# Hash projection on eighths of the matmul array, weight rounding one unit ahead, and a third buffer for loaded q and k

## The chip, the cores and the metric

The kernel runs on one core of a Trainium2 chip. The metric is the device time of one execution in microseconds. Before the change the median of three runs is 935.21 us (933.5 to 935.66).

## The reference

The program is an attention block with a hash mask, followed by an MLP. In NumPy, cut to what matters:

```python
# q, k, v: (4, 8, 768, 64) float32; proj: (64, 6)
q_bits = einsum(q, proj) > 0;  k_bits = einsum(k, proj) > 0     # 6 bits per row
mask   = bucket(q_bits)[:, :, :, None] == bucket(k_bits)[:, :, None, :]
attn   = softmax(where(mask, q @ k.T / 8, -1e9));  y = attn @ v
x = y.transpose(0, 2, 1, 3).reshape(3072, 512)
h = x @ w_in                                   # w_in (512, 2048)
out = (max(h, 0) + alpha * min(h, 0)) @ w_out  # w_out (2048, 512)
```

A query row attends to the key rows whose six hash bits all agree with its own. The MLP weights arrive as 64-bit floats and are rounded to float32 in the kernel.

## The kernel before, in words

**Two stages.** The attention stage takes the first 370 us or so; the MLP stage takes the rest. In the attention stage the 32 heads of the batch are taken as 16 pairs (`pi`), and each pair as two units (`u = 2 * pi + g`, with `g` 0 or 1 for the half of the 384 query columns). The loop at L1002 runs over the 32 units. Every engine's order is the order of the program (`do` at L439 keeps it), so an instruction that has to wait holds up everything behind it on its engine. Which DMA is issued when on a queue is left to the scheduler.

**One unit on TensorE.** `scores` (L687) runs six key chunks: three for the second half of unit `u`, and then three for the first half of unit `u + 1`. Each chunk is a bf16 product of hash bits and a float32 product of q and k, added in PSUM (L696), for the two heads `s` of the pair; each head occupies 64 rows of the array. After them comes either `hash_bits(pi + 1)` (L1016, in units with `g == 0`) or the transposes of q and k for pair `pi + 2` (`turn`, L1018 and L1019, in units with `g == 1`). Then comes the first half of `attend` (L729), `totals` (L741), and the second half of `attend`.

**Where the PSUM results go.** ScalarE takes the exponential of every score chunk (L701), copies the transposes (L648), writes the hash bits as signs (L676), takes the absolute value of a weight piece for rounding (`weight_abs`, L558) and sums squares of q and k (`magnitude`, L657). VectorE sums probabilities over key chunks (L710, L715, L716, L719; one of the six chunks is added by a DMA, L711), does the rounding of one weight piece per unit (`weight_parts`, L564 to L569, `weight_sum`, L589 and L594), the sums of weight blocks that the MLP's Strassen products need (`weight_sums`, L614), and the division (`divide`, L751 to L757). `totals` on TensorE needs L719 of its unit. `divide` needs `totals` and both halves of `attend`.

**The hash.** `hash_bits` (L659) multiplies the 6-column projection with the transposed q and k of both heads. The weight of head `s` (`wh[s]`, L457) has 128 rows, of which the 64 rows of the other head are zero. A product therefore uses all 128 rows and 32 columns of the array. For each half of the 768 columns there are four products: k and q of head 0, k and q of head 1. They land in the four 32-partition groups of one PSUM bank.

```python
r = D * s + 32 * n
do(PE.matmul(ps[r : r + 32, half, :CW], wh[s],
             tr[name, pi][:, half * CW : (half + 1) * CW], start=True, stop=True))
```

**Weights.** There are 32 pieces (`NW`), one rounded per unit. In unit `u` the kernel rounds piece `u`: `weight_abs(u)` stood at the end of the unit before, `weight_parts(u)` stands ahead of the first half of `attend`, and `weight_sum(u)` after `totals`. Pieces form groups; when a group is complete (`weight_group`) four sums and a store to DRAM are queued, and `weight_sums` takes one or two of them per unit. In the last unit `weight_sums(4)` (L1028) takes what is left. The first MLP activations are written by L849 into a pool that takes the place of the attention stage's pool in SBUF, so this write has to wait for the last readers of what lay there.

**Loads.** `load` (L479) fetches q, k and v of a pair. The tiles for q and k rotate over two buffers; the load for pair `pi + 2` overwrites what `magnitude(pi)` has just read. L1044 to L1050 place the magnitudes and the loads that follow them. All of these loads, the weight pieces and most stores are issued on the SyncE queue.

Of the kernel before, what the change touches and what calls it, by code (L numbers as in the profile page):

```python
# [404 lines left out]
def fast_path(  # L405
# [48 lines left out]

    ident = const.tile([P, P], F32, name="ident")
    ones = const.tile([P, D], F32, name="ones")
    wh = [const.tile([P, 32], F32, name=f"wh{s}") for s in range(2)]  # L457
    hb = const.tile([P, 1], F32, name="hb")
    alpha16 = const.tile([NF, P], F32, name="alpha16")
    alpha = const.tile([P, NF], F32, name="alpha")  # L460
# [18 lines left out]
    def load(pi, name):  # L479
        b, hp = pairs[pi]  # L480
        src = {"q": q, "k": k, "v": v}[name]
        if name == "v":
            t = pool.tile([P, 2, NC * D], F32, name=f"vn{pi}", tag="vn")
            nc.sync.dma_start(t, src[b, 2 * hp : 2 * hp + 2].rearrange("h (p c) d -> p h (c d)", c=NC))
            nat[name, pi] = t
        else:
            load_part(pi, name, slice(0, NC), nc.sync)

    def load_part(pi, name, cs, queue):
        b, hp = pairs[pi]  # L490
        src = {"q": q, "k": k}[name]
        if cs.start == 0:
            nat[name, pi] = pool.tile([P, NC, 2, D], F32, name=f"{name}n{pi}", tag=f"{name}n")
        for s in range(2):
            queue.dma_start(nat[name, pi][:, cs, s], src[b, 2 * hp + s].rearrange("(p c) d -> p c d", c=NC)[:, cs])

    def setup():

        zero = const.tile([P, 512], BF16, name="zero")
        do(DVE.memset(zero, 0.0))  # L500
        for s in range(2):
            do(DVE.memset(wh[s], 0.0))
            nc.sync.dma_start(wh[s][D * s : D * s + D, :NB], proj)
        nc.sync.dma_start(alpha16, moe_alpha.rearrange("(t p) -> t p", p=P))
        make_identity(nc, ident)
        do(DVE.memset(ones, 1.0))

        ps = psum.tile([P, 512], F32, name="nil", tag="av")
        for i in range(12):
            do(PE.matmul(ps, zero[:, :P], zero, start=True, stop=True))  # L510

        do(DVE.memset(hb, 0.0))
        for r in range(0, P, 32):
            do(DVE.memset(hb[r : r + 2 * NB], 1.0 if r % D else -1.0))
            do(DVE.memset(hb[r : r + NB], -1e-37))
# [39 lines left out]
    def weight_abs(i):  # L555
        lo, hi = halves(i)
        wx[i] = pool.tile([P, 512], F32, name=f"wx{i}", tag="wx")
        do(ACT.activation(wx[i], hi.bitcast(F32), AF.Abs))  # L558

    def weight_parts(i):  # L560
        lo, hi = halves(i)
        x = wx[i]
        wr[i] = r = pool.tile([P, 512], F32, name=f"wr{i}", tag="wr", bufs=1)
        do(DVE.tensor_scalar(x, x, HI_MIN, None, op0=ALU.max, op1=ALU.max, accum_out=wmax[:, i : i + 1]))  # L564
        do(DVE.tensor_scalar(
            x.bitcast(U32), x.bitcast(U32), 3, 0xC0000000, op0=ALU.logical_shift_left, op1=ALU.bitwise_xor,
        ))
        do(DVE.tensor_scalar(r.bitcast(U32), x.bitcast(U32), 0x7F800000, None, op0=ALU.bitwise_and))
        do(DVE.scalar_tensor_tensor(r, lo, 2.0 ** -52, r, op0=ALU.mult, op1=ALU.mult))  # L569

    def weight_sum(i):


        lo, hi = halves(i)
        x, r = wx[i], wr[i]
        if i < HW:
            n, m = divmod(i, 4)
            if m == 0:
                wst[n] = pool.tile([P, NM, 4, P], F32, name=f"wsi{n}", tag="wsi")
# [79 lines left out]
    def hash_bits(pi, halves=BOTH):  # L659


        if halves.start == 0:
            bits["q", pi] = qbs[pi % 2]
            bits["k", pi] = pool.tile([P, S], BF16, name=f"kb{pi}", tag="kb")
        ps = two_banks(f"hs{pi}")
        for half in range(halves.start, halves.stop):
            for s in range(2):
                for n, name in enumerate("kq"):
                    r = D * s + 32 * n
                    do(PE.matmul(  # L670
                        ps[r : r + 32, half, :CW], wh[s], tr[name, pi][:, half * CW : (half + 1) * CW],
                        start=True, stop=True,
                    ))

        def sign(t, rows, ps_rows):
            do(ACT.activation(  # L676
                t[rows].rearrange("p (h w) -> p h w", h=2)[:, halves], ps[ps_rows, halves, :CW], AF.Sign,
                bias=hb[ps_rows],
            ))

        for s in range(2):
            sign(bits["q", pi], slice(D * s, D * s + 32), slice(D * s + 32, D * s + D))

        sign(bits["k", pi], slice(0, P), slice(0, P))


    def scores(u, half):  # L687
        pi, g = divmod(u, NCH)
        qs = slice(g * CW, (g + 1) * CW)
        for kc in range(half * NC // 2, (half + 1) * NC // 2):  # L690
            sc = two_banks(f"sc{u}_{kc}")
# [9 lines left out]
            do(ACT.activation(pt[:, :, :CW], sc[:, :, :CW], AF.Exp, scale=SCALE / DOWN))  # L701
            prob[u, kc] = pt
# [290 lines left out]
    for i in range(1, 3):  # L993
        load_weight(i)
    load(1, "v")
    scores(0, 0)
    add_first(0)
    hash_bits(0, second)
    for name in "qk":
        turn(1, name)  # L1000
    weight_abs(0)
    for u in range(UNITS):  # L1002
        pi, g = divmod(u, NCH)
        scores(u, 1)
# [12 lines left out]
        if g == 1 and pi + 2 < NPAIR:  # L1017
            turn(pi + 2, "q")  # L1018
            turn(pi + 2, "k")  # L1019
        weight_parts(u)  # L1020
        attend(u, 0)
        totals(u)
        weight_sum(u)
        weight_sums(1 if u < HW else 2)
        weight_group(u)
        attend(u, 1)
        if u == last:
            weight_sums(4)  # L1028
        divide(u)
        if g == 1 and pi + 2 < NPAIR:  # L1030
            load(pi + 2, "v")
        load_weight(u + 3)
        if u == HW + 2:
            load_w(0)
            load_w(1)
            load_x(0)
        if HW + 4 <= u < HW + 8:
            sum_x(0, u - HW - 4, DVE)
        if u + 1 < NW:
            weight_abs(u + 1)  # L1040
        if u == 1:
            setup_alpha()

        done = [(u, "q"), (u, "k")] if u < 2 else []  # L1044
        if 2 <= pi + 1 + g < NPAIR:
            done.append((pi + 1 + g, "kq"[g]))
        for p2, name in done:
            magnitude(p2, name)
            if p2 + 2 < NPAIR:
                load(p2 + 2, name)  # L1050


    late = []
# [83 lines left out]
```

## Time and profile before

The page of the profile shows these engines over the span of 932.4 us:

| engine | busy us | share |
|---|---|---|
| TensorE, matmul | 916.9 | 98% |
| VectorE | 756.1 | 81% |
| ScalarE | 399.6 | 43% |
| GpSimd | 40.9 | 4% |

The busy share is an average over stages. In the 40 slices of the span VectorE shows 9 tenths or more from slice 3 to slice 15, which is the attention stage, and ScalarE shows 6 to 8 tenths up to slice 14. In the MLP stage ScalarE falls to 1 to 3 tenths. The chain of work that ended last is 92% TensorE, 3% VectorE, 2% ScalarE and 1% DMA. A busy TensorE record is modelled and overlaps its neighbour: a float32 product of 384 columns is shown as 0.49 us, but such records follow each other every 0.325 us. The distance between starts is therefore the figure to use.

A pair of regular units takes 22.13 us in the chain. The unit from 306.09 to 317.15 us holds the scores (4.95 us), the hash (1.43 us), half of `attend` (2.09 us), the totals (0.65 us) and the other half (1.94 us).

### The profile page before, as it was taken

To read this page: it belongs to the slowest core of one execution; us is meant where nothing else is said; L and a number is where in the kernel's file an instruction comes from. 1 tells how busy PE (TensorE), PEld (TensorE's weight loads), DVE (VectorE), ACT (ScalarE), POOL (GpSimd) and SP (SyncE) were. 2 spreads that over 40 slices of the span, in tenths; PEclk is the share of its full clock that TensorE was granted. 3 is DMA by queue.
4 is the path that set the end of the run, shared out by engine and by line. 5 is a ranking of instruction groups with operands and counts; after the bars stand their busy time and mean duration, and the time that the engine had idled before them with its cause. 6 is when DMAs were issued, how large, how long until landed. Compare 5 with 4: busy or idle time off the path is not lost.

```text
span 932.4 us, 13579 instructions
## 1 busy us (share of the span) xinstructions
PE 916.9 (98%) x5073; PEld 610.5 (65%) x5073; DVE 756.1 (81%) x1317; ACT 399.6 (43%) x690; POOL 40.9 (4%) x50
## 2 busy tenths in 40 slices
PE   8999999999999999899999999999999999999996
PEld 4444444444454444556999556998556998556996
DVE  2889999999999999677978667988667988677985
ACT  6877777777777763222122222122222112322212
POOL 1111111111111110000000000000000000000000
PEclk9999999999999999999999999999999999999999
DMA  7876888989877563634424334334234334231231
GB/s 187 191 177 159 218 204 208 268 211 234 220 187 187 153 165 99 236 102 147 146 109 153 112 119 142 135 108 169 96 118 152 126 115 162 98 116 40 94 133 71
DMA packets 114062, 141.50 MB, mean 152 GB/s; under 512 B 54067, under 2 KB 102211, under 8 KB 110403
## 3 DMA queue, kind: packets, MB, share of 16 engines
q1 hardware_dynamic: 103680, 127.56, 43.2%
q0 software_dynamic: 8704, 12.58, 8.3%
q8 instruction: 42, 0.69, 0.3%
q10 hardware_dynamic: 1600, 0.39, 0.2%
q14 instruction: 36, 0.27, 0.1%
HBM read 100.67 MB, written 27.26 MB: 137 GB/s over the span
## 4 chain that ended last, share of the span: by engine, by line
PE 92%; DVE 3%; ACT 2%; DMA 1%; issue 1%; SPq 0%; DVEq 0%; ACTq 0%
PE sc L696 15%; PE av L729 12%; PE hs L670 2%; PE z_4a L803 2%; PE z_5a L803 2%; PE z_7a L803 2%; PE z_3a L803 2%; PE z_1a L803 2%; PE z_6a L803 2%; PE z_2a L803 2%; PE f_5a L803 2%; PE f_7a L803 2%; PE f_3a L803 2%; PE f_4a L803 2%; PE f_2a L803 2%; PE f_6a L803 2%
## 5 line engine op out<-in xcount | busy, mean ns | idle before, releaser
L701 ACT ACTIVATE pt<-sc 128x768 f32<-128x768 f32 x192 | 152.9, 814 | 78.5 <-PE sc L696 76.6
L696 PE MATMUL sc<-qT,kT 64*128 64x384 f32 x768 | 155.1, 483 | 0.0
L729 PE MATMUL av<-pt,vn 128*64 128x385 f32 (+1 forms) x768 | 136.5, 491 | 0.0
L729 PEld LDWEIGHTS av<-pt,vn 128*64 128x64 f32 x768 | 52.3, 136 | 70.7 <-issue 61.2
L696 PEld LDWEIGHTS sc<-qT,kT 64*128 64x128 f32 x768 | 68.2, 188 | 34.8 <-issue 34.4
L853 DVE TENSOR_TENSOR g<-g,g 128x384 f32<-128x384 f32 x128 | 68.4, 555 | 2.2
L696 PE MATMUL sc<-qb,kb 64*128 64x384 bf16 x384 | 63.0, 325 | 1.6 <-ACT kb L676 1.5
L893 DVE TENSOR_TENSOR ws<-wl 128x512 f32<-128x512 f32 x56 | 38.5, 688 | 23.4 <-DMA wl<-w_out_s 23.4
L901 DVE TENSOR_TENSOR gs<-g,gs 128x768 f32<-128x768 f32 x56 | 53.5, 955 | 1.0
L901 DVE TENSOR_TENSOR gs<-g 128x768 f32<-128x768 f32 x56 | 53.4, 953 | 0.0
L711 POOL DMA_DIRECT2D accp<-pt x32 | 38.5, 1204 | 317.0 <-DVE accp L710 189.4
L849 DVE SCALAR_TENSOR_TENSOR g<-h,alpha 128x384 f32<-128x384 f32 x32 | 19.8, 618 | 35.3 <-ACT h L842 35.3
L696 PEld LDWEIGHTS <-kb 64*128 64x128 bf16 x384 | 19.2, 94 | 41.7 <-issue 18.4
L715 DVE TENSOR_TENSOR accd<-pt,pt 128x768 f32<-128x768 f32 x32 | 30.6, 956 | 14.1 <-ACT pt L701 14.0
L710 DVE TENSOR_TENSOR accp<-pt,pt 128x768 f32<-128x768 f32 x32 | 30.4, 952 | 11.3 <-ACT pt L701 11.3
L716 DVE TENSOR_TENSOR accd<-accd,pt 128x768 f32<-128x768 f32 x32 | 30.7, 958 | 3.3
L676 ACT ACTIVATE qb<-hs,hb 32x768 bf16<-32x768 f32 (+1 forms) x34 | 29.1, 855 | 10.0 <-PE hs L670 8.7
L719 DVE TENSOR_TENSOR accd<-accd,accp 128x768 f32<-128x768 f32 x32 | 30.6, 958 | 1.1
L913 DVE TENSOR_TENSOR m<-m,m 128x768 f32<-128x768 f32 (+1 forms) x40 | 28.6, 716 | 1.9 <-ACT m L919 1.2
L741 PE MATMUL sm<-accd,ones 128*64 128x384 f32 x128 | 26.2, 487 | 0.3 <-DVE accd L719 0.3
L670 PE MATMUL hs<-kT,wh 128*32 128x384 f32 x128 | 24.1, 492 | 0.6 <-ACT kT L648 0.6
L670 PE MATMUL hs<-qT,wh 128*32 128x384 f32 x128 | 24.2, 492 | 0.0
(323 smaller groups left out, 1794.1 us busy)
## 6 DMA issues: line engine op xcount, KB each, us to landing
wi<-w_in_s SPq DMA_DIRECT2D x32, 896.0 KB, 4.5
wl<-w_out_s SPq DMA_DIRECT2D x28, 1024.0 KB, 4.8
accp<-pt POOLq DMA_DIRECT2D x32, 384.0 KB, 4.4
raw<-in_moe_w_in_dram SPq DMA_DIRECT2D x16, 512.0 KB, 4.2
raw<-in_moe_w_out_dram SPq DMA_DIRECT2D x16, 512.0 KB, 4.0
w_in_s<-wsi SPq DMA_DIRECT2D x16, 448.0 KB, 5.7
w_out_s<-wso SPq DMA_DIRECT2D x8, 896.0 KB, 5.7
vn<-in_v_dram SPq DMA_DIRECT2D x16, 384.0 KB, 5.1
```

Source lines behind the costliest of these rows:

```text
L670: do(PE.matmul(ps[r : r + 32, half, :CW], wh[s], tr[name, pi][:, half * CW : (half + 1) * CW], start=True, stop=True,))
L696: do(PE.matmul(sc[:, s, :CW], what["k", pi][r, ks], what["q", pi][r, qs], start=first, stop=not first,))
L701: do(ACT.activation(pt[:, :, :CW], sc[:, :, :CW], AF.Exp, scale=SCALE / DOWN))
L711: nc.gpsimd.dma_start(accp[u], p(u, 2), accum_op=ALU.add)
L715: do(DVE.tensor_tensor(accd[u], p(u, 3), p(u, 4), op=ALU.add))
L716: do(DVE.tensor_tensor(accd[u], accd[u], p(u, 5), op=ALU.add))
L719: do(DVE.tensor_tensor(accd[u], accd[u], accp[u], op=ALU.add))
L729: do(PE.matmul(av[u][D * s : D * s + D, :w], nat["v", pi][:, s, kc * D : (kc + 1) * D], prob[u, kc][:, s, :w], start=(kc == 0), stop=(kc = ...
L803: do(PE.matmul(self.ps[bank], self.left(left, k), self.right(right, k), start=start and k == 0, stop=k == self.nk - 1, skip_group_check=no ...
L853: do(DVE.tensor_tensor(new_g(b, to)[:, i], g_m[b, x][:, i], g_m[b, y][:, i], op=ALU.subtract))
L893: do(DVE.tensor_tensor(t, w2[b, n, x], w2[b, n, y], op=op))
L901: do(DVE.tensor_tensor(t, g2[b, n, x], g2[b, n, y], op=ALU.subtract))
```

## The change

The change has three parts.

1. **Hash on eighths.** One weight tile `wh` holds the projection in rows 0 to 63 and again in rows 64 to 127. A product takes 64 rows and 32 columns. The output columns are shifted by half an array for the second half of the data (`s ^ half`), so that the eight products of a pair have eight different places. The signs are then taken half by half: three activations for the first half, four for the second, where k is written in two pieces because its two heads have changed places.
2. **Rounding a piece ahead.** Piece 0 is rounded ahead of the loop; unit `u` rounds piece `u + 1`. The last unit rounds nothing and takes the four remaining sums at the place where it rounded before.
3. **Three buffers for q and k.** The loads for pair 2 are issued ahead of the loop. In the loop both magnitudes of pair `pi` and both loads of pair `pi + 3` come at the end of the unit with `g == 1`.

```diff
-    wh = [const.tile([P, 32], F32, name=f"wh{s}") for s in range(2)]
+    wh = const.tile([P, 32], F32, name="wh")
...
-            nat[name, pi] = pool.tile([P, NC, 2, D], F32, name=f"{name}n{pi}", tag=f"{name}n")
+            nat[name, pi] = pool.tile([P, NC, 2, D], F32, name=f"{name}n{pi}", tag=f"{name}n", bufs=3)
...
-            for s in range(2):
-                for n, name in enumerate("kq"):
-                    r = D * s + 32 * n
+            for n, name in enumerate("kq"):
+                for s in range(2):
+                    r, c = D * s, D * (s ^ half) + 32 * n
                     do(PE.matmul(
-                        ps[r : r + 32, half, :CW], wh[s], tr[name, pi][:, half * CW : (half + 1) * CW],
+                        ps[c : c + 32, half, :CW], wh[r : r + D], tr[name, pi][r : r + D, half * CW : (half + 1) * CW],
                         start=True, stop=True,
                     ))
-        for s in range(2):
-            sign(bits["q", pi], slice(D * s, D * s + 32), slice(D * s + 32, D * s + D))
-        sign(bits["k", pi], slice(0, P), slice(0, P))
+        for half in range(halves.start, halves.stop):
+            cols = slice(half * CW, (half + 1) * CW)
+            for s in range(2):
+                c = D * (s ^ half) + 32
+                do(ACT.activation(
+                    bits["q", pi][D * s : D * s + 32, cols], ps[c : c + 32, half, :CW], AF.Sign, bias=hb[c : c + 32],
+                ))
+            for to, c, n in [(0, 0, P)] if half == 0 else [(0, D, D), (D, 0, D)]:
+                do(ACT.activation(
+                    bits["k", pi][to : to + n, cols], ps[c : c + n, half, :CW], AF.Sign, bias=hb[c : c + n],
+                ))
...
     load(1, "v")
+    load(2, "q")
+    load(2, "k")
     scores(0, 0)
     add_first(0)
     hash_bits(0, second)
+    weight_abs(0)
+    weight_parts(0)
+    weight_sum(0)
+    load_weight(3)
     for name in "qk":
         turn(1, name)
-    weight_abs(0)
+    weight_abs(1)
...
-        weight_parts(u)
+        if u < last:
+            weight_parts(u + 1)
+        else:
+            weight_sums(4)
         attend(u, 0)
         totals(u)
-        weight_sum(u)
-        weight_sums(1 if u < HW else 2)
-        weight_group(u)
+        if u < last:
+            weight_sum(u + 1)
+            weight_sums(1 if u < HW - 1 else 2)
+            weight_group(u + 1)
         attend(u, 1)
-        if u == last:
-            weight_sums(4)
         divide(u)
...
-        load_weight(u + 3)
+        load_weight(u + 4)
...
-        if u + 1 < NW:
-            weight_abs(u + 1)
+        if u + 2 < NW:
+            weight_abs(u + 2)
...
-        done = [(u, "q"), (u, "k")] if u < 2 else []
-        if 2 <= pi + 1 + g < NPAIR:
-            done.append((pi + 1 + g, "kq"[g]))
-        for p2, name in done:
-            magnitude(p2, name)
-            if p2 + 2 < NPAIR:
-                load(p2 + 2, name)
+        if g == 1:
+            for name in "qk":
+                magnitude(pi, name)
+                if pi + 3 < NPAIR:
+                    load(pi + 3, name)
```

More of the change, by code (lines that the diff above doesn't have):

```diff
@@ L500, in setup @@
         do(DVE.memset(zero, 0.0))
+        do(DVE.memset(wh, 0.0))
         for s in range(2):
-            do(DVE.memset(wh[s], 0.0))
-            nc.sync.dma_start(wh[s][D * s : D * s + D, :NB], proj)
+            nc.sync.dma_start(wh[D * s : D * s + D, :NB], proj)
         nc.sync.dma_start(alpha16, moe_alpha.rearrange("(t p) -> t p", p=P))
@@ L666, in hash_bits @@
         for half in range(halves.start, halves.stop):
-            for s in range(2):
-                for n, name in enumerate("kq"):
-                    r = D * s + 32 * n
+            for n, name in enumerate("kq"):
+                for s in range(2):
+                    r, c = D * s, D * (s ^ half) + 32 * n
                     do(PE.matmul(
-                        ps[r : r + 32, half, :CW], wh[s], tr[name, pi][:, half * CW : (half + 1) * CW],
+                        ps[c : c + 32, half, :CW], wh[r : r + D], tr[name, pi][r : r + D, half * CW : (half + 1) * CW],
                         start=True, stop=True,
                     ))
[L675 to L679, printed above, removed]
-        for s in range(2):
-            sign(bits["q", pi], slice(D * s, D * s + 32), slice(D * s + 32, D * s + D))
-        sign(bits["k", pi], slice(0, P), slice(0, P))
+        for half in range(halves.start, halves.stop):
[9 more added lines that the diff above has]
+                ))
     def scores(u, half):
```

## The prediction

> **What bounds the kernel now.** I read the page first (engines, groups), then the chain of waits, and then the timelines of TensorE and VectorE in the attention stage. From the page:
>
> ```profile
> PE 916.9 (98%) x5073; PEld 610.5 (65%) x5073; DVE 756.1 (81%) x1317; ACT 399.6 (43%) x690; POOL 40.9 (4%) x50
> ...
> L670 PE MATMUL hs<-kT,wh 128*32 128x384 f32 x128 | 24.1, 492 | 0.6 <-ACT kT L648 0.6
> L670 PE MATMUL hs<-qT,wh 128*32 128x384 f32 x128 | 24.2, 492 | 0.0
> ```
>
> TensorE is nearly full. The 256 hash records belong to 128 products: a float32 product is recorded as two passes. The timeline of TensorE for the hash of pair 15:
>
> ```profile
> 333.10 0.51 PE L670 MATMUL hs<-kT,wh 128*32 128x384 f32 x1
> 333.11 0.51 PE L670 MATMUL hs<-qT,wh 128*32 128x384 f32 x1
> 333.12 0.51 PE L670 MATMUL hs<-kT,wh 128*32 128x384 f32 x1
> 333.12 0.51 PE L670 MATMUL hs<-qT,wh 128*32 128x384 f32 x1
> ...
> 333.45 0.49 PE L670 MATMUL hs<-kT,wh 128*32 128x384 f32 x1
> ...
> 333.77 0.49 PE L670 MATMUL hs<-kT,wh 128*32 128x384 f32 x1
> ...
> 334.10 0.49 PE L670 MATMUL hs<-kT,wh 128*32 128x384 f32 x1
> ...
> 334.53 2.16 PE L729 MATMUL av<-pt,vn 128*64 128x385 f32 x12
> ```
>
> The four column places start together, in four rounds (two halves, two passes), and the next work starts 1.43 us after the hash began. The timeline of VectorE, each unit's first sum L715 (units 19, 20, 21, 30, 31):
>
> ```profile
> 231.30 0.96 DVE L715 TENSOR_TENSOR accd<-pt,pt 128x768 f32<-128x768 f32 x1 [0.24 <-ACT pt L701]
> 242.37 0.96 DVE L715 TENSOR_TENSOR accd<-pt,pt 128x768 f32<-128x768 f32 x1
> 253.96 0.95 DVE L715 TENSOR_TENSOR accd<-pt,pt 128x768 f32<-128x768 f32 x1
> ...
> 352.56 0.95 DVE L715 TENSOR_TENSOR accd<-pt,pt 128x768 f32<-128x768 f32 x1
> 363.14 0.95 DVE L715 TENSOR_TENSOR accd<-pt,pt 128x768 f32<-128x768 f32 x1
> ```
>
> At unit 19 VectorE waits for its input; from unit 20 to 31 it waits only 0.25 us more, at 341.96. So VectorE is a second bound, just below TensorE. The end of the stage, and the one stall of its start:
>
> ```profile
> 33.26 0.85 PE L647 MATMUL tp_q<-ident,qn 128*128 128x128 f32 x6 [0.89 <-DMA qn<-in_q_dram]
> ...
> 366.20 0.87 PE L741 MATMUL sm<-accd,ones 128*64 128x384 f32 x4 [0.29 <-DVE accd L719]
> ...
> 377.69 0.62 DVE L849 SCALAR_TENSOR_TENSOR g<-f_0u,alpha 128x384 f32<-128x384 f32 x1 [2.70 <-DMA w_out_s<-wso]
> ...
> 379.95 1.56 PE L803 MATMUL f_1b<-x,wi 128*128 128x384 f32 x4 [3.01 <-DVE f_0p L845]
> ```
>
> In the last unit VectorE finishes its weight piece and six sums, the last store goes out at 372.27, L849 waits for it, and TensorE stands 3.01 us.
>
> **What the Trainium skill says.** "TensorE: Matmul & The Clock Gate", Part 3 (packing small matmuls), says that row and column places combine, and that a packed group takes the time of one product plus some ns per place. The trace agrees for each direction alone: four column places in one round of 0.325 us (hash), and two row places in one round (L696, 64 rows each, two records of 0.33 us). It shows no case of both. "PSUM — Partial Sum Buffer", PSUM bank collisions, says that two row places must not write one bank within one group of 32 partitions at a time, while different groups are free. By the diff, the two heads of one half write opposite halves of the partitions, so all eight may run; no run here shows it yet. "DMA: Bandwidth & Descriptors", Issuing engines are not separate DMA queues, says that all issued transfers interleave on the same 16 engines. The page agrees that they share: the mean DMA share is 0.6 to 0.9 in most attention slices.
>
> **The hash.** After the change there are two rounds: 0.35 us to the second, and 0.43 us from the last round to the next work (334.10 to 334.53), together 0.78 us. Bounds: 0.70 us (twice 0.35), and 1.43 us if nothing is gained. I take 0.78, a saving of 0.65 us for each of pairs 1 to 15. Pair 0 is hashed half by half, four products at a time as before: nothing.
>
> **The signs.** Before, three activations of 768 columns take 2.6 us (69.09 to 71.71). After, seven of 384: at 14.26 two q signs take 1.17 us to the next start and the k sign 0.48, so 4 x 0.585 + 3 x 0.5 = 3.8 us. This adds 1.2 us to ScalarE in units with g = 0, but the magnitude (0.8 us) leaves them. ScalarE ends the exponentials 5.9 us after the unit's first score; plus 3.8 and 0.6 (weight_abs) is 10.3, and its next score chunk is ready 10.4 + 1.1 after. It fits by about a microsecond. In units with g = 1 it now has two magnitudes: 5.9 + 1.5 (copies) + 0.6 + 1.7 = 9.7 against 11.1 + 1.1. No cost in either.
>
> **The start.** In the first unit ScalarE is the limit: the scores at 18.72 wait for the exponential at 17.84. Ahead of it come one more sign (0.5) and one more weight_abs (0.55): +1.1 us. VectorE rounds piece 0 in 4.98 us in which it was idle: nothing. The loads of pair 2 go out before the loop; the DMA stands empty from 20 to 25 us, so 0.8 MB more arrives by about 23, and the transposes that started at 33.26 find them. Unit 1 took 13.1 us (27.35 to 40.45) against 11.07 plus 0.16 for alpha: saves 1.87. Sum at unit 2, with one hash: -1.87 + 1.1 - 0.65 = -1.42 us.
>
> **TensorE alone.** Fourteen more hashes: 14 x 0.65 = 9.1. With the start 1.42, the wait at 366.20 (0.29) and the stall (3.01), TensorE alone would give 13.8: 921.4 us.
>
> **VectorE.** Its work per unit is the same, one piece shifted. Its pace without waits is 10.54 us in the w_in part (22.13 less the waits of 0.58, 0.24 and 0.22, halved), 10.6 in the w_out part (352.56 to 363.14), and 11.5 in units 20 to 23 with the sums of x. TensorE's mean unit becomes 11.07 - 0.33 = 10.74. So VectorE keeps up until unit 20, about 0.5 us late after the two units with two large sums (198.11 to 220.38, 11.13 each). Then it loses 0.7 per unit for four units. TensorE can bear 2 us in a g = 0 unit: L715 comes 2.7 us after the first score when on time; totals come at 4.95 + 0.78 + 2.09 = 7.8, and need L715 3.05 earlier, at 4.75. And units 29 to 31 have neither hash nor transposes (9.62 us between scores, 339.21 to 348.83), so VectorE sets the pace to the end. From L715 of unit 20 to that of unit 31 it needs 363.14 - 242.37 - 0.25 = 120.5 us. L715 of unit 20 moves from 242.37 by 1.42 and nine hashes (5.85), plus 0.5 late: 235.6. L715 of unit 31: 356.1; its L719 ends 3.0 later at 359.1, where it was 366.15: 7.05 us gained.
>
> **The end.** After L719 only four sums (1.7 us) remain ahead of the division, and the store leaves near 361 and lands, at 5.3 us, near 366.3. L849 wants to start near 365.5; it may wait 1 us, but TensorE needs its result only at 369.9. The stall of 3.01 us goes. Sum 10.06: 935.21 - 10.06 = 925.2 us. The MLP stage is untouched.
>
> **The added waits.** The loads of pair pi + 3 now leave at the end of an odd unit and are needed 16 us later, against a landing time of 5.0 us (k is behind a store on the queue, some 4 us later). Behind a late transpose stand attend and totals, and so VectorE. I cost it at nothing, with 3 us to spare.
>
> **The rivals.** (1) VectorE doesn't bind, since its pace has slack that I count as work: 921.4 us. Against it: no waits from 242 us on. (2) The eight places don't overlap more than four at a time, hash 1.43 us: start -0.77, stall -3.01, so 931.4 us. For it: no trace of both directions. (3) Slower: the row places exclude each other in the narrow form, with two column places at a time: 16 passes in 8 rounds of 0.325 are 2.7 us with the tail, +1.27 x 15 = 19, less 3.8: 950 us; or loads late by 1 us or more in each of 13 turns, some 938 us. Against the first: L696's two row places start together; against the second: the 16 us.
>
> **How the numbers follow.** VectorE bound, 925.2: 0.66. TensorE alone, 921.4: 0.12. No gain of the hash, 931.4: 0.13. Slower: 0.09. The range from 920.5 to 932 takes in the first three with the bounds of the hash, and leaves out the last and a little more. Faster by over 0.2% (933.3): 0.89; within: 0.03; slower: 0.08.
>
> **What would show it.** Hash records in two rounds of eight with the next work 0.7 to 0.8 us after; no DMA wait at the transposes of unit 1; VectorE without waits from unit 20 on, and totals waiting for L719 in some of them; no 3 us stall at f_1b. Hash rounds of four or two, waits for q or k, or ScalarE holding the scores would make it wrong.

## The result, and the profile after

The changed kernel takes 924.24 us (median of 5 runs, 923.43 to 925.64), where the kernel before takes 935.21 us (933.5 to 937.06). The ratio is 0.9887, with a 95% interval from 0.9868 to 0.9905: a gain of 10.97 us, where 10.0 was forecast. Measured a second time, beside runs of before of its own, it is 924.45 against 934.22 (0.9891, 0.9872 to 0.9909), a gain of 9.8 us.

The page of the profile after, engines and the chain that ended last:

```profile
PE 907.8 (98%) x5073; PEld 605.4 (66%) x5073; DVE 754.0 (82%) x1316; ACT 422.6 (46%) x751; POOL 40.9 (4%) x50
...
PE 65%; DVE 16%; DMA 2%; issue 1%; ACT 0%; DVEq 0%; ACTq 0%
```

TensorE has 9.1 us less busy time, ScalarE 23 us more (the extra signs), VectorE about the same (754.0 and 756.1). The shares of busy time say little here. The chain says more: VectorE carries 16% of it (11% in a second profile of the changed kernel), where it carried 3% before. In the groups of TensorE, the hash keeps its 256 records, but their busy time falls from 48.3 us to 29.2:

```profile
L671 PE MATMUL hs<-kT,wh 64*32 64x384 f32 x128 | 14.6, 495 | 0.6 <-ACT kT L648 0.6
L671 PE MATMUL hs<-qT,wh 64*32 64x384 f32 x128 | 14.6, 495 | 0.0
```

One record is as long as before (495 ns against 492), so the gain is overlap alone. The timeline of TensorE for one hash shows it (start, duration, engine, line, operands, records in the entry):

```profile
66.32 0.51 PE L671 MATMUL hs<-kT,wh 64*32 64x384 f32 x2
66.34 0.51 PE L671 MATMUL hs<-qT,wh 64*32 64x384 f32 x2
66.35 0.51 PE L671 MATMUL hs<-kT,wh 64*32 64x384 f32 x2
66.36 0.51 PE L671 MATMUL hs<-qT,wh 64*32 64x384 f32 x2
66.67 0.49 PE L671 MATMUL hs<-kT,wh 64*32 64x384 f32 x2
...
67.13 0.55 PE L731 MATMUL av<-pt,vn 128*64 128x385 f32 x2
```

Two rounds of eight records, at 66.32 and 66.67, and the next work after 0.81 us (67.13 - 66.32) instead of 1.43.

The timeline of VectorE in the kernel after, the first sums of units 20, 21, 30 and 31 (L717 was L715 before):

```profile
237.53 0.95 DVE L717 TENSOR_TENSOR accd<-pt,pt 128x768 f32<-128x768 f32 x1
248.98 0.95 DVE L717 TENSOR_TENSOR accd<-pt,pt 128x768 f32<-128x768 f32 x1
...
346.95 0.95 DVE L717 TENSOR_TENSOR accd<-pt,pt 128x768 f32<-128x768 f32 x1
357.54 0.95 DVE L717 TENSOR_TENSOR accd<-pt,pt 128x768 f32<-128x768 f32 x1
```

No entry has a wait. VectorE's last wait is in fact in unit 12, at 154.34 us (it is shown further below), and from there to 360 us it runs at its own pace, eight units earlier than forecast. TensorE has room until unit 22. From 263.51 us on it is TensorE that waits for VectorE. Its timeline in the start of the stage, in these units and at the end (L743 was L741, L805 was L803):

```profile
32.49 0.87 PE L647 MATMUL tp_q<-ident,qn 128*128 128x128 f32 x6
...
263.51 0.87 PE L743 MATMUL sm<-accd,ones 128*64 128x384 f32 x4 [0.38 <-DVE accd L721]
...
350.00 0.87 PE L743 MATMUL sm<-accd,ones 128*64 128x384 f32 x4 [0.75 <-DVE accd L721]
360.59 0.87 PE L743 MATMUL sm<-accd,ones 128*64 128x384 f32 x4 [0.39 <-DVE accd L721]
...
371.17 1.13 PE L805 MATMUL f_1b<-x,wi 128*128 128x384 f32 x3
```

The transposes of pair 2 no longer wait for their load, the totals wait for VectorE's L721 in five units after unit 20 (the two that are not shown are 0.16 us at 274.97 and 0.81 at 286.44; before there was one such wait, at the very end), and `f_1b` starts without the 3.01 us stall.

To place the gain, the attention stage is cut at marks that both kernels have: the first transposes, VectorE's first sums of units 2, 20 and 31, and `f_1b`. The time ahead of the first transposes differs from run to run of one kernel (5.2 us in one profile of the changed kernel, 5.7 in the other), so it is left out of the first column. All in us, each row one profile:

| kernel | transposes to unit 2 | 2 to 20 | 20 to 31 | 31 to `f_1b` | `f_1b` to the end |
|---|---|---|---|---|---|
| before | 36.84 | 199.24 | 120.77 | 16.81 | 552.5 |
| after | 37.43 | 194.92 | 120.01 | 13.63 | 552.7 |
| after, second profile | 35.52 | 194.93 | 119.99 | 13.64 | 552.3 |

The MLP stage is the same. The gain is in the hash (2 to 20), in the end (31 to `f_1b`), and, in the second profile, in the start.

### The profile page after: what moved, and what is told of

Read it like the earlier page. It is cut to its first block, busy times and chain, and to the rows that moved or that the text cites. A ratio compares the mean times of both kernels' runs of the same rounds, so it can differ in the third digit from the quotient of the medians.

```text
span 923.9 us, 13627 instructions
## 1 busy us (share of the span) xinstructions
PE 907.8 (98%) x5073; PEld 605.4 (66%) x5073; DVE 754.0 (82%) x1316; ACT 422.6 (46%) x751; POOL 40.9 (4%) x50
## 4 chain that ended last, share of the span: by engine, by line
PE 65%; DVE 16%; DMA 2%; issue 1%; ACT 0%; DVEq 0%; ACTq 0%
PE sc L698 3%; PE z_4a L805 2%; PE f_4a L805 2%; PE z_7a L805 2%; PE z_5a L805 2%; PE z_3a L805 2%; PE z_6a L805 2%; PE z_2a L805 2%; PE z_1a L805 2%; PE f_2a L805 2%; PE f_5a L805 2%; PE f_7a L805 2%; PE f_6a L805 2%; PE f_1a L805 2%; PE av L731 2%; PE f_0a L805 2%
## 5 line engine op out<-in xcount | busy, mean ns | idle before, releaser
L713 POOL DMA_DIRECT2D accp<-pt x32 | 38.5, 1204 | 311.4 <-DVE accp L712 150.2
L851 DVE SCALAR_TENSOR_TENSOR g<-h,alpha 128x384 f32<-128x384 f32 x32 | 19.8, 618 | 36.0 <-ACT h L844 36.0
L679 ACT ACTIVATE qb<-hs,hb 32x384 bf16<-32x384 f32 x64 | 36.7, 574 | 2.2 <-issue 1.1
L721 DVE TENSOR_TENSOR accd<-accd,accp 128x768 f32<-128x768 f32 x32 | 30.7, 958 | 5.1 <-DMA accp<-pt 4.1
L717 DVE TENSOR_TENSOR accd<-pt,pt 128x768 f32<-128x768 f32 x32 | 30.5, 952 | 3.6 <-ACT pt L703 3.6
L743 PE MATMUL sm<-accd,ones 128*64 128x384 f32 x128 | 26.5, 492 | 3.2 <-DVE accd L721 3.1
L684 ACT ACTIVATE kb<-hs,hb 64x384 bf16<-64x384 f32 (+1 forms) x48 | 27.7, 578 | 0.6
L564 DVE TENSOR_SCALAR_CACHE_REDUCE wx<-wx 128x512 f32<-128x512 f32 x32 | 21.7, 679 | 2.9 <-ACT wx L558 2.9
```

What stands on the lines that cost most here:

```text
L679: do(ACT.activation(bits["q", pi][D * s : D * s + 32, cols], ps[c : c + 32, half, :CW], AF.Sign, bias=hb[c : c + 32],))
L713: nc.gpsimd.dma_start(accp[u], p(u, 2), accum_op=ALU.add)
L717: do(DVE.tensor_tensor(accd[u], p(u, 3), p(u, 4), op=ALU.add))
L721: do(DVE.tensor_tensor(accd[u], accd[u], accp[u], op=ALU.add))
```

## Experiments

### Each part alone

The three parts of the change were each put alone into the kernel before: `hash_only` is part 1 of the diff above, `ahead_only` part 2, `buffers_only` part 3.

> The kernel before with the hash change alone (one weight tile, 64 rows, shifted columns, seven signs). Theory V (VectorE is the second bound and sets the end of the attention stage): nine hashes of 0.62 us saved up to unit 20 are 5.6 us, less 0.5 us that VectorE is late by then, less about 1.5 us at the start, because one more sign and 1.2 us of signs stand ahead of the magnitude that frees the buffer for the loads of pair 2; the stall of 3.0 us at the end stays: 931.5 us. Theory P (TensorE alone): 15 hashes of 0.62 us, less 1.5 us at the start, and the stall stays: 927.5 us. A third theory (the eight places do not overlap): 935 to 937 us, hash rounds four as before.

> The kernel before with the rounding one piece ahead alone. Theories V and P alike: one more absolute value ahead of the first exponentials costs 0.55 us, the stall of 3.0 us at the first product of the second MLP block goes: 932.7 us. If the stall moves elsewhere instead (the first activations wait for the store anyway): 935 us or more.

> The kernel before with the third buffer for q and k and the moved magnitudes and loads alone. Theories V and P alike: the wait for the loads of pair 2 in unit 1 goes, 1.9 us: 933.3 us. If the loads bunched in the odd units disturb the accumulating transfer (its landing above 8.5 us in some unit, with VectorE waiting for it): 934 to 936 us.

| kernel | us (range, runs) | before | ratio (95%) | transposes to unit 2 | 2 to 20 | 20 to 31 | 31 to `f_1b` | sum against before |
|---|---|---|---|---|---|---|---|---|
| hash_only | 932.05 (929.37 to 932.83, 8) | 934.20 | 0.9972 (0.9959 to 0.9984) | 37.74 | 194.70 | 119.99 | 16.80 | -4.4 |
| ahead_only | 932.15 (931.01 to 934.72, 13) | 934.20 | 0.9978 (0.9970 to 0.9987) | 37.46 | 199.25 | 120.94 | 13.63 | -2.4 |
| buffers_only | 935.64 (933.08 to 938.8, 22) | 934.20 | 1.0012 (1.0003 to 1.0021) | 36.75 | 200.85 | 120.76 | 16.84 | +1.5 |

`hash_only` and `ahead_only` came within 0.6 us of 931.5 (theory V) and 932.7. `buffers_only` missed its 933.3 and fell in the range named for a disturbed accumulating transfer; the longest landing of one in its profile is 10.2 us.

Each part does its own job. The hash alone takes 4.5 us out of the stretch from unit 2 to 20 and leaves the stall at `f_1b` (3.00 us) as it was. Rounding ahead alone takes out the stall (3.18 us) and nothing from the middle. The third buffer alone brings nothing at the start: the chain there is held by other waits (an accumulating transfer, 2.98 us at 23.02). It costs 1.6 us between 2 and 20, where the transposes of k now wait for their loads at 167.11 (0.24 us) and 234.50 (0.43 us) and VectorE's L719 waits 0.72 us at 178.40.

But the parts don't add up to the whole. Their timed gains are 2.15, 2.05 and -1.44, together 2.8 us of about 10. So two of the parts were joined.

### The first two parts together

The kernel `hash_ahead` is the changed kernel without part 3.

> The kernel before with the hash change and the rounding ahead, without the third buffer. If the parts add up as each was measured alone (2.2 us for the hash, 2.0 us for the rounding): 930 us against before at 934.2. If the rounding ahead brings its full 3.0 us stall on top of what the profile of the hash alone shows (4.8 us): 926.5 us. If the wait for the loads of pair 2 is what held the hash back, the third buffer is worth 2 to 3 us here though it costs alone: about 927 us, against 924 us with it.

It takes 926.69 us (925.66 to 927.15, 6 runs) against 934.30: 0.9913 (0.9895 to 0.9932), a gain of 7.6 us. The third buffer is therefore worth another 2 us or so in this company (0.9913 against 0.9887 and 0.9891, that is 2.1 to 2.4 us of 934.3), although alone it is a small loss. The timeline of TensorE in `hash_ahead` shows what it removes:

```profile
33.28 0.85 PE L647 MATMUL tp_q<-ident,qn 128*128 128x128 f32 x6 [0.60 <-DMA qn<-in_q_dram]
...
35.67 1.37 PE L647 MATMUL tp_k<-ident,kn 128*128 128x128 f32 x6 [1.54 <-DMA kn<-in_k_dram]
```

Without the third buffer the loads of pair 2 are late, by 2.14 us in two waits, and the way to unit 2 takes 39.88 us; with it, 35.52 to 37.43. But not all of the 39.88 is the loads: `hash_only` has the same two waits (0.62 and 1.60 us) and takes 37.74. Behind the waits the clock granted to TensorE fell in the profile of `hash_ahead`, and it did not in that of `hash_only`. The view by windows of both, from 35 to 40 us, `hash_ahead` first (length, then the engines' busy time; the last three figures are the granted clock, where 1 is full speed, the DMA share and GB/s):

```profile
35.00:40.00 5.00, 4.33 (x18) 2.29 (x20) 3.18 (x7) 2.92 (x7) 1.20 (x1) 0.66 0.58 106
35.00:40.00 5.00, 4.67 (x30) 2.41 (x32) 3.78 (x8) 3.78 (x8) 0.96 (x1) 1.00 0.68 125
```

The transposes of k and the half of `attend` behind them take 1.37 and 3.26 us in `hash_ahead`, and 0.84 and 2.16 in `hash_only`: the clock took 1.6 us. From 2 to 20 `hash_ahead` is faster than the changed kernel (193.84 us against 194.92); it has no wait for an accumulating transfer there.

In the profiles parts 1 and 2 come close to adding up: -4.4 and -2.4 alone, and together 39.88 + 193.84 + 119.98 + 13.64 = 367.34 us from the first transposes to `f_1b`, where before has 373.66: -6.3, with the 1.6 us of slow clock in it. In the timed medians they do not (2.15 + 2.05 = 4.2 alone, 7.6 together).

What differs is the clock. The mean clock of every timed run is known, and within `hash_only`, and within the kernel before, the runs at the lowest clocks are the longer ones. Four runs of `hash_only` at 0.994 or 0.995 take 932.5 us on average, two at 0.998 take 929.5. Of the 38 runs of before beside them, two at 0.995 take 937.1 and eighteen at 0.998 take 933.8. At 0.998 on both sides the hash alone gains 4.4 us, as in its profile. The kernels that keep the stall (`hash_only`, `buffers_only`, before) go down to 0.994, the changed kernel only to 0.997. A mean of 0.997 alone is no sign of lost time: in the profile of `after_spread` (further below), which has that mean, the clock is under 1.00 only behind the last product. The stall can't be the only cause, since `ahead_only`, which has none, has four runs at 0.996.

One profile shows the clock falling at the stall. It is of `buffers_only`, the view by windows of 10 us:

```profile
370.00:380.00 10.00, 7.25 (x23) 3.92 (x21) 6.92 (x17) 0.96 (x2) 0.00 (x0) 0.97 0.66 218
380.00:390.00 10.00, 9.71 (x21) 5.48 (x22) 5.79 (x11) 1.83 (x5) 0.00 (x0) 0.69 0.68 287
```

After a stall of 3.04 us that ended at the start of this second window the clock is 0.69, and the rest of the kernel takes 555.3 us instead of 552.5. The Trainium skill says the same: "TensorE: Matmul & The Clock Gate", Why this matters for your kernels, advises against gaps of more than about 3 us between bursts of products, since the clock falls after one. The trace agrees here, but it doesn't in every execution: in the profile of before the window 380 to 390 shows 1.00 after a stall of 3.01 us. Nor does it take a gap of 3 us: in `hash_ahead` the clock fell behind waits of 0.60 and 1.54 us. Where in a timed run the clock fell is not known, so that the stall is what slows the timed runs of the kernels that keep it is argued, and not shown. If it is so, taking the stall away was worth more than its 3 us.

### The eight places, or only the 64 rows

In `no_shift` the changed kernel keeps its narrow products (64 rows, one weight tile), but both halves of the data use the same places. It computes the same thing.

```diff
-                    r, c = D * s, D * (s ^ half) + 32 * n
+                    r, c = D * s, D * s + 32 * n
...
-                c = D * (s ^ half) + 32
+                c = D * s + 32
-            for to, c, n in [(0, 0, P)] if half == 0 else [(0, D, D), (D, 0, D)]:
+            for to, c, n in [(0, 0, P)] if half == 0 else [(0, 0, D), (D, D, D)]:
```

> The kernel after, but the output columns are not shifted for the second half of the data: again 64 rows and 32 columns for each product and seven signs, but only four different places, each used twice. If the eight different places make the gain: four rounds again, 1.43 us to the next work, and 931 to 934 us. If the gain came from the halved rows themselves: two rounds, 0.8 us, and 924 us as after.

It takes 929.64 us (929.34 to 930.33, 5 runs) against 934.20: 0.9949 (0.9936 to 0.9961). This is 5.4 us slower than the changed kernel. The timeline of TensorE in `no_shift`, one hash:

```profile
65.97 0.51 PE L671 MATMUL hs<-kT,wh 64*32 64x384 f32 x2
...
66.96 0.49 PE L671 MATMUL hs<-kT,wh 64*32 64x384 f32 x2
...
67.39 0.54 PE L731 MATMUL av<-pt,vn 128*64 128x385 f32 x2
```

Four rounds again (the two that are left out start at 66.31 and 66.64), and 1.42 us to the next work. The time lies in neither of the two ranges that were expected; the rounds decide between them. Halving the rows saves no round by itself. The shift, which gives the eight products eight different places, saves both. From unit 2 to 20 `no_shift` takes 199.17 us, as before (199.24). The 5.4 us is less than 15 hashes by 0.62 us (9.3), and more than half of the difference is the second bound: in the stretch 20 to 31 TensorE saves 5 hashes, 3.1 us, but the stage gains only 0.75 (120.75 to 120.01).

### VectorE with less to do

The forecast rests on VectorE setting the pace from unit 20 on. If it does, a shorter VectorE shortens the changed kernel there, and does much less for the kernel before. Both kernels were run without one instruction of the rounding, which is 0.69 us in each unit. They leave out the scaling of the low word that the rounding needs, so the weights are wrong in them.

```diff
-        do(DVE.scalar_tensor_tensor(r, lo, 2.0 ** -52, r, op0=ALU.mult, op1=ALU.mult))
```

> The kernel after with one VectorE instruction of the rounding left out (the product with the low word, 0.73 us in each of 32 pieces, so the rounding loses its correction term). Theory V: VectorE's pace falls from 10.5 to 9.8 us a unit, under TensorE's mean of 10.75, no total waits for it any more, and the time falls to what TensorE alone gives: 0.987 of before less 2.5 to 3 us, about 921 to 922 us against before at 934 to 935. Theory P: VectorE has room anyway, so nothing changes: 0.9887 of before, 924 us.

> The kernel before with the same VectorE instruction left out: the control. Theories V and P: TensorE bounds it up to the last units; gained are 0.3 us of wait for the last totals and 0.7 us of the last piece ahead of the stall, 1.0 us: 933.2 us against 934.2. If VectorE had bounded the kernel before all along: 3 us or more.

| kernel | us (range, runs) | before | ratio (95%) | transposes to unit 2 | 2 to 20 | 20 to 31 | 31 to `f_1b` |
|---|---|---|---|---|---|---|---|
| after_light | 920.27 (919.47 to 922.06, 5) | 934.30 | 0.9852 (0.9831 to 0.9873) | 35.54 | 193.97 | 116.22 | 14.58 |
| before_light | 931.19 (929.98 to 933.25, 14) | 934.30 | 0.9968 (0.9957 to 0.9979) | 35.92 | 199.24 | 119.32 | 16.06 |

In the stretch 20 to 31 the changed kernel falls from 120.0 to 116.2 us, none of TensorE's totals waits for VectorE any more, and VectorE waits for its input again. Its timeline in `after_light` (L716 is L717):

```profile
299.23 0.96 DVE L716 TENSOR_TENSOR accd<-pt,pt 128x768 f32<-128x768 f32 x1 [1.11 <-ACT pt L702]
309.66 0.96 DVE L716 TENSOR_TENSOR accd<-pt,pt 128x768 f32<-128x768 f32 x1 [0.24 <-ACT pt L702]
```

And 116.2 is about what TensorE alone needs: 119.32 us in `before_light`, less 5 hashes of 0.62, is 116.2. So the bound of VectorE in these units is shown: it is 3.8 us above that of TensorE.

The control missed its forecast: it gained 3.1 us timed, where 1.0 was expected, and 3 us or more had been named for a VectorE that bounds the kernel before all along. It doesn't bound it all along: that would give 22 us (32 units by 0.69), and the gain is nothing from 2 to 20. It is 1.45 from 20 to 31, 0.75 at the end, and 0.9 at the start. The 2.2 us behind unit 20 are VectorE's way to the last store. In the kernel before it has one wait of 0.25 us from unit 20 to that store, and with less work the stall at `f_1b` falls from 3.01 to 1.32 us. So VectorE's pace already set the end of the attention stage in the kernel before, through the stall. The gain at the start needs another explanation, since VectorE isn't the pace there. The timeline of the SyncE queue in the kernel before (start and duration of the issue):

```profile
27.09 0.33 SPq L546 DMA_DIRECT2D raw<-in_moe_w_in_dram  x1
27.54 1.24 SPq L495 DMA_DIRECT2D qn<-in_q_dram  x2
```

The load of pair 2 stands behind the load of weight piece 3. This takes over the buffer of piece 0, and so waits for the last instruction that reads it, VectorE's L594 (26.34 to 27.03). The wait at 33.26 us in the kernel before was therefore not for the buffer of q alone: it was for the place in the queue, and so for VectorE. With a lighter VectorE the two loads leave at 26.02 and 26.67, and unit 2 comes 0.9 us earlier.

### Off VectorE: the block sums on GpSimd

If VectorE is the bound, giving work away should help. `weight_sums` is some 0.9 us a unit, and GpSimd is idle. First all of it was moved, as it stands:

```diff
-            do(DVE.tensor_tensor(w[:, to], w[:, a], w[:, c], op=op))
+            do(POOL.tensor_tensor(w[:, to], w[:, a], w[:, c], op=op))
```

> The kernel after with the sums of weight blocks moved from VectorE to GpSimd, all work kept. Theory V: VectorE loses 0.6 to 0.8 us a unit from unit 3 on, as in the run with the instruction left out, and TensorE alone sets the time: 921 to 922 us. Theory P: 924 us. A rival of its own: GpSimd's sums slow VectorE down or delay the accumulating transfer that GpSimd issues: 925 us or more.

It takes 950.15 us (949.79 to 950.86, 5 runs) against 934.30: 1.0167 (1.0146 to 1.0188). It is slower by 26 us than the changed kernel, and by 16 than the kernel before. The stretch 20 to 31 rises to 129.85 us. The groups of VectorE in the changed kernel, one line:

```profile
L568 DVE TENSOR_SCALAR wr<-wx 128x512 uint32<-128x512 uint32 x32 | 13.9, 436 | 1.1
```

And the same line in `after_pool`:

```profile
L568 DVE TENSOR_SCALAR wr<-wx 128x512 uint32<-128x512 uint32 x32 | 55.9, 1748 | 1.1
```

One instruction of the rounding went from 436 to 1748 ns, and the one behind it (L569) from 692 to 938, because the sums of GpSimd now ran beside them: 0.88 us saved in each unit, 1.31 + 0.25 = 1.56 lost. The Trainium skill has this in "SBUF — State Buffer", Who interferes with whom: VectorE and GpSimd share a pair of ports. A `tensor_scalar`, as L568 is, can run in a mode that takes the pair, and whichever engine has it keeps it for a whole instruction, while the other stands; a VectorE operation with two SBUF inputs, as L569 is, meets a GpSimd operation that reads SBUF. The two durations agree with both statements. The other cause that had been named, a late accumulating transfer, is not what happened: the profile shows no wait of VectorE for one. A sum of 128x512 takes 1.68 us on GpSimd here, and one of 128x256 0.99.

So the sums were put away from these two operations: behind L594, the last step of the unit's rounding. A one-column sum on GpSimd, which reads the piece that L594 has just written, holds them back (`newest` is a column of that piece). The four sums of the last unit stay on VectorE.

```diff
+        if sums_due and newest and count < 4:
+            do(POOL.tensor_tensor(tick, newest[0], newest[0], op=ALU.add))
+        engine[0] = POOL if count < 4 else DVE
...
-            do(DVE.tensor_tensor(w[:, to], w[:, a], w[:, c], op=op))
+            do(engine[0].tensor_tensor(w[:, to], w[:, a], w[:, c], op=op))
```

> The kernel after with the sums of weight blocks on GpSimd, but each unit's sums start only when VectorE has written the unit's weight piece (a one-element operation on GpSimd reads that piece first), so that they lie beside the division and the additions and not beside VectorE's bitwise operations on the words; the last four sums stay on VectorE. All work kept. If the slow-down with the sums on GpSimd came from the one bitwise operation that took 1.75 us instead of 0.44: that operation is back at 0.44, VectorE loses 0.7 to 0.8 us a unit, and TensorE alone sets the time, 920.5 to 922 us. If GpSimd's work slows every VectorE operation beside it: 930 us or more.

In the groups of `pool_late` the blocked instruction, L568, is short again: 454 ns. But the conflict has in part moved. The sums now lie beside the division, and its small `tensor_scalar` of 12 columns is long, here in the changed kernel and in `pool_late`:

```profile
L754 DVE TENSOR_SCALAR rc<-st 128x12 f32<-128x12 f32 x32 | 5.6, 174 | 1.1
L762 DVE TENSOR_SCALAR rc<-st 128x12 f32<-128x12 f32 x32 | 19.6, 612 | 1.1
```

So VectorE gets back about half of the 0.88 us of the sums, and not the 0.7 to 0.8 us expected. A sum of 128x512 takes 1.26 us, and the stretch 20 to 31 takes 116.68 us, close to the 116.2 of TensorE alone. This shows the bound a second time, now with the whole computation. The profiled span is 918.4 us, against 922.1 in the second profile of the changed kernel, taken beside it. The timed runs don't confirm that it is the faster kernel: 923.32 us (920.64 to 925.57, 6 runs), where 920.5 to 922 was forecast, against 924.45, ratios to before of 0.9883 (0.9864 to 0.9903) and 0.9891 (0.9872 to 0.9909). The intervals lie on each other. Its runs scatter by 5 us, with the longest two at mean clocks of 0.996 and 0.997 and the shortest at 0.999, and the gain of the profile is not established.

### The missed wait in units 11 and 12

The stretch 2 to 20 gained 4.3 us, where the forecast had nine hashes less half a microsecond (5.4). The timeline of VectorE in the changed kernel has two waits there that the kernel before has not:

```profile
146.77 0.69 DVE L594 SCALAR_TENSOR_TENSOR wsi<-raw,wr 128x512 uint32<-128x512 uint32 x1 [0.81 <-DMA w_in_s<-wsi]
...
154.34 0.96 DVE L721 TENSOR_TENSOR accd<-accd,accp 128x768 f32<-128x768 f32 x1 [2.04 <-DMA accp<-pt]
```

And the chain that ended last in the first profile of the changed kernel, in order of time, has this as its longest piece (the chain of the second profile doesn't pass through it):

```profile
143.51 10.74 DMA accp<-pt
```

The accumulating transfer that adds one of the six chunks (L713) usually lands in 4.3 us. Here it takes 10.7. From 138 to 158 us the 16 DMA engines are full by the profile's measure, with a mean of 330 GB/s. Four stores of 448 KB (`w_in_s`, from 136.89) and two loads of weights with 896 KB each (`wi`, 142.49) were issued ahead of the transfer at 143.51. A weight piece of 512 KB, q, v and k of a pair came behind it, q at 147.91 and k at 152.69. Two kernels test what the transfer and the paired loads have to do with the wait. `after_spread` is the changed kernel with one load in each unit instead of two in every second one:

```diff
-        if g == 1:
-            for name in "qk":
-                magnitude(pi, name)
-                if pi + 3 < NPAIR:
-                    load(pi + 3, name)
+        name = "kq"[g]
+        magnitude(pi, name)
+        if pi + 3 < NPAIR:
+            load(pi + 3, name)
```

> The kernel after with three buffers, but the magnitude and load of k in the unit with g = 0 and those of q in the unit with g = 1, so that a unit loads one of them. If the loads bunched in the odd units are what makes the accumulating transfer late around 143 to 154 us (2 to 3 us of VectorE): 922 to 923 us. If the stores and loads of weight blocks make it late: 924 us. If ScalarE, with signs and a magnitude in one unit, now holds the scores: 926 us or more.

`after_noacc` leaves the accumulating transfer out, so its sums lack one chunk of six:

```diff
-        nc.gpsimd.dma_start(accp[u], p(u, 2), accum_op=ALU.add)
```

> The kernel after without the accumulating transfer of GpSimd (one of six key chunks is left out of the sum of probabilities, so the sums are too small): VectorE has the same instructions, but never waits for that transfer. Theory V: the 2.0 us that VectorE waited at 154 us, when it no longer had slack, come back, and a little less traffic: 921.5 to 922.5 us. If the wait was absorbed by slack: 924 us.

The changed kernel was run once more beside them:

> The kernel after itself, beside the three others of this call, so that they can be compared with it on one chip. Every theory: 0.989 of before, 924 us.

| kernel | us (range, runs) | ratio to 934.22 (95%) | transposes to unit 2 | 2 to 20 | 20 to 31 | 31 to `f_1b` | `f_1b` to the end |
|---|---|---|---|---|---|---|---|
| after_again | 924.45 (923.61 to 924.92, 5) | 0.9891 (0.9872 to 0.9909) | 35.52 | 194.93 | 119.99 | 13.64 | 552.3 |
| after_spread | 924.50 (923.66 to 925.42, 5) | 0.9895 (0.9877 to 0.9913) | 35.73 | 193.40 | 120.02 | 13.63 | 553.5 |
| after_noacc | 923.24 (923.07 to 923.98, 5) | 0.9879 (0.9860 to 0.9897) | 35.54 | 193.61 | 119.93 | 13.63 | 552.9 |

The wait is in both profiles of the changed kernel (2.04 and 2.15 us). It is gone in `after_spread` and `after_noacc`, and from unit 2 to 20 both take 1.3 to 1.5 us less. So the late transfer costs this stretch about that much. That the paired loads are what makes it late is not shown. The timeline of VectorE in `hash_only`, which has two buffers and no paired loads there, has the same wait:

```profile
165.72 0.96 DVE L721 TENSOR_TENSOR accd<-accd,accp 128x768 f32<-128x768 f32 x1 [2.03 <-DMA accp<-pt]
```

And `after_spread`, which doesn't have it, moves as much from 138 to 158 us (326 GB/s). It also changes the order: its `wi` loads are issued behind the transfer (143.23 and 141.97) and not ahead of it. What makes the transfer late stays open.

In the timed runs the wait doesn't come back as gain: `after_spread` (922 to 923 forecast if the paired loads were the cause) is as fast as the changed kernel, and `after_noacc` (921.5 to 922.5 forecast) 1.2 us faster, with intervals that overlap. In their profiles the part behind `f_1b` is 1.2 and 0.6 us longer. This lies behind the last products, which start 545.6 us after `f_1b` in all three profiles: there only the last copy and store are left. Why the timed runs show no gain is not settled.

## Why the prediction was right

The forecast was 925.2 us in a range from 920.5 to 932; measured were 924.24 and 924.45. The likeliest case came true: VectorE becomes the bound. It runs without a wait from unit 12 on, where unit 20 was forecast, and TensorE waits for it from unit 22 on.

- **The hash: right.** Two rounds of eight, 0.81 us to the next work, against 0.78 forecast. `no_shift` shows that the different places do it. That row and column places combine, as the skill's page on packing says, is what the trace shows, now for both directions at once. Two row places, in different groups of 32 partitions of one bank, also run together: the four products of one half share a bank, and all eight start within 0.04 us. The rival of 931.4 us, in which the eight don't overlap, is what `no_shift` built: 929.64.
- **The signs: right.** ScalarE has 23 us more busy time, but after the first 20 us TensorE never waits for it in the attention stage.
- **The start: the size was near, a part of the cause was wrong.** Forecast was -1.42 us at unit 2. Six profiles with all three parts (`after_again`, `after_light`, `after_pool`, `pool_late`, `after_spread`, `after_noacc`) lie 1.1 to 1.3 us below before. The profile taken for the result lies 0.6 above: the accumulating transfer of unit 0 was late there, and VectorE's L721 waited 2.02 us for it at 23.79, TensorE's totals 0.58 and alpha's product 1.02 after it. The only other profile with such a wait of over a microsecond there is that of `buffers_only` (2.98 us), and both kernels load pair 2 ahead of the loop; that these loads make the transfer late is not shown, and other kernels with them have 0.6 us or less. The step put the price of the early loads at nothing. It also said that the load waited for the buffer. `before_light` showed that it waited for its place in the queue behind a weight piece too.
- **TensorE alone, 921.4 us: not reached,** as forecast. `after_light`, where VectorE has room, gives 920.27, a microsecond from that figure.
- **VectorE as second bound: right, and the central step.** From unit 20 to unit 31 120.0 us were measured in every kernel with the new hash and the whole of VectorE's work, 120.5 forecast. Its two tests, less work (116.2) and work moved away (116.7), both free the stretch.
- **"About 0.5 us late" at unit 20: too small.** This term of the sum missed the waits in units 11 and 12. From 2 to 20 the forecast was 5.85 less 0.5, and 4.3 were measured; without the accumulating transfer's wait it is 5.6 to 5.8. The step on added waits held where it looked: no transpose in the changed kernel waits for q or k. It looked at the instructions that need these loads, and not at what else is in flight, although the prediction had drawn on the skill's statement that all issued transfers interleave on the same engines.
- **The end: right.** 16.81 us became 13.63, a gain of 3.18 against 3.01 for the stall. L851 doesn't wait for the last store any more (its first instance starts at 366.93). The forecast had the last L721 end at 359.1; it ended at 360.5 in one profile and at 359.2 in the other.

The misses partly cancelled: by the second profile the sum from the first transposes to `f_1b` is 1.3 + 4.3 + 0.8 + 3.2 = 9.6 us, where 10.06 was forecast; the timed gains are 11.0 and 9.8. That the three parts alone give so much less (2.8 us timed, 5.3 in the profiles) wasn't foreseen. The runs show two reasons: the third buffer pays only where the loads of pair 2 hold the start, and the clock falls behind waits in some executions. The second is shown in two profiles, and for the timed runs it is argued.

## What to carry to other kernels

When the bound engine gets faster, find the engine just below it, and in which units it has no waits: the gain there is the distance between the two paces, and not the work saved. Follow a load not only to who needs it, but to what stands ahead of it on its queue and to what else is in flight when it is. And moving work to an idle engine is no gift where the two share ports: look at the instructions that will run at the same time, wherever the work is put.

## What the runs showed of the hardware

- Eight float32 products of 64 rows and 32 columns, in eight different places of the array and two PSUM banks, run side by side: a pass of all eight is one round (0.35 us to the next), and two passes take two rounds. The same eight in four places take four rounds. So the number of different places counts, and not the number of rows.
- VectorE's bitwise operation on 128x512 words takes 436 ns alone and 1748 ns on average with GpSimd's sums beside it; a `tensor_scalar` of only 12 columns went from 174 to 612 ns. GpSimd's sum of 128x512 takes 1.26 us beside the division and 1.68 us beside the rounding.
- An accumulating transfer of 4.3 us took 10.7 us while the DMA engines were full, at 330 GB/s. In another kernel, at 326 GB/s, none was waited for.
- After a stall of TensorE of 3.04 us its granted clock was 0.69 over the next 10 us in one profile, and 1.00 after one of 3.01 us in another. After two waits of 0.60 and 1.54 us it was 0.66 over 5 us in one profile, and 1.00 after 0.62 and 1.60 us in another.
